# Squares of two row tiles and masks of a whole head pair at a time, six blocks by seven products, a ring of three, and copies off GpSimd, in a fused sparse attention and feed-forward kernel

**Chip and metric.** One core of one Trainium2 chip. Times are device microseconds (us) of whole executions; a profile's span runs from its first to its last instruction and is 1 to 2 us shorter.

## The reference

```python
# q, k, v: (8 batches, 8 heads, 576, 64);  w_in: (512, 2048);  w_out: (2048, 512)
scores = q @ k^T / 8                     # heads 0..3 see the last 32 positions ("loc"),
scores = where(mask[head], scores, -1e9) # heads 4..7 every 32nd one ("str")
x = (softmax(scores) @ v) as (4608, 512)
out = (s * relu(x @ w_in)**2 + b) @ w_out    # fp32
```

## The kernel before

All 4608 rows go through the feed-forward part in nine blocks T of 512. The first product (4 x 16 matmuls of 512 columns a block) gives a bank of PSUM for each of 16 row tiles; ScalarE takes the relu into `u`, VectorE squares it into `gT`. The second product comes in two forms: plain, 64 matmuls of 512 columns, or, from block `SEVEN` on, a 2 x 2 blocked product by seven products instead of eight, 112 matmuls of 256 columns, which needs sums of parts of `gT` (VectorE), mixed weights (made once) and more evictions. Attention of batch b runs between these matmuls and writes its transposed result into `xT`, a ring of `NX` batches.

A planner in Python simulates the engines when the program is built. It fixes the order of each engine's instructions, and for a copy it chooses the engine that it thinks will end first. Each `post` names what it needs, a cost in ns for each engine that may do it ("A" ScalarE, "V" VectorE, "P" GpSimd, "D" a transposing DMA), the function and the keys it sets. Each engine then works through its own instructions in that order; the GpSimd timeline of `e2_before_seven3` below shows a copy that stands behind DMA issues.

```python
LAT = {"A": 70.0, "V": 70.0, "P": 70.0, "D": 12000.0, ...}
...
eng = min(p[1], key=lambda e: max(self.free[e], r) + p[1][e])       # who ends first
...
    # scores of a bank: exponential, then its mask (84 masks in all)
    s.posts = [([key], {"A": 170 + 0.83 * 2 * n * nq}, ex, [("e", id_, g), group]),
               ([("e", id_, g)], {"V": 150 + 0.52 * 2 * n * nq}, ms, [("p", id_, g)])]
...
    # spreading q^T of the strided heads over qD_str
    plan.post([("qT", id_), ("s", (b - 1, m), 2)], {"P": 2000.0, "V": 940.0, "A": 1340.0},
              q_spread, [("q", id_)])
...
    # GpSimd issues the loads of batch b + 2; the plan counts no time for it
    plan.post([...], {"P": 0.0}, lambda eng, b=b: fetch_qk(b + 2), [("fetch", b + 2)])
    plan.post([...], {"P": 0.0}, lambda eng: fetch_v(b + 2), [("fetch_v", b + 2)])
```

The softmax here doesn't subtract the row's maximum and nothing guards it: scores larger than these inputs give would overflow.

## Time and profile before

| kernel before | |
|---|---|
| time | 311.52 us, median of 3 (311.32 to 311.59); profiled run 310.75, span 309.0 |
| busy: TensorE / VectorE / ScalarE / GpSimd | 97% / 71% / 58% / 32% |
| TensorE waits that the profile lists | 4.0 us, 2.6 of them before 21 us |

The prediction below shows and reads the profile's lines.

### The profile page before, as it was taken

The numbers are of one execution on the slowest core, as the hardware profiler recorded it, in microseconds if no ns is written. First come the engines' busy times: TensorE is split into PE (matmuls) and PEld (weight loads), VectorE is DVE, ScalarE is ACT, GpSimd is POOL, SyncE is SP. The second block draws the span as 40 slices with busy tenths as digits, with TensorE's granted clock in tenths as the row PEclk, the third lists the DMA queues.
The fourth block names the chain that finished last, engine by engine and source line by source line (L and its number), as shares of the span: only waits on it lengthen the run. The fifth ranks groups of instructions, "written<-read, shape, count | busy, mean of one in ns | idle before, by whom it ended". The sixth has DMA issues, their size and how long they took to land.

```text
span 309.0 us, 6715 instructions
## 1 busy us (share of the span) xinstructions
PE 300.5 (97%) x2526; PEld 194.4 (63%) x2526; DVE 218.2 (71%) x575; ACT 178.3 (58%) x336; POOL 99.8 (32%) x146
## 2 busy tenths in 40 slices
PE   8899999989999999999999999999999999999994
PEld 3765655555656655556687755565677666766883
DVE  7567958799976877859755874589866366737653
ACT  1876945769736964668055736694945445356300
POOL 8562559934951592059202950000000000000000
PEclk9999999999999999999999999999999999999999
DMA  7999999998999699679998999842010100200313
GB/s 127 204 212 205 216 175 159 219 135 122 99 165 176 86 147 155 110 110 183 150 174 153 128 146 159 172 92 88 2 36 34 68 2 34 104 1 0 105 67 106
DMA packets 99940, 37.28 MB, mean 121 GB/s; under 512 B 81170, under 2 KB 95890, under 8 KB 99906
## 3 DMA queue, kind: packets, MB, share of 16 engines
q0 software_dynamic: 57200, 18.08, 60.9%
q1 hardware_dynamic: 42706, 18.76, 29.9%
q8 instruction: 20, 0.33, 0.5%
q14 instruction: 14, 0.11, 0.1%
HBM read 36.84 MB, written 10.32 MB: 153 GB/s over the span
## 4 chain that ended last, share of the span: by engine, by line
PE 82%; DMA 9%; DVE 4%; issue 2%; ACT 1%; POOL 1%; SPq 0%; DVEq 0%; POOLq 0%; ACTq 0%
PE ps_f L877 35%; PE ps_f L926 20%; PE ps_f L845 12%; DMA ql<-in_q_dram 6%; PE ps_s L531 4%; PE ps_a L585 2%; DMA w_out_sb<-in_v_dram 2%; PE ps_s L845 2%; PE ps_t L585 1%; PE ps_t L845 1%; PE ps_s L926 1%; PE ps_t L411 1%; DMA out_dram<-o 1%; PE ps_t L633 1%; DVE gT L908 1%
## 5 line engine op out<-in xcount | busy, mean ns | idle before, releaser
L877 PE MATMUL ps_f<-xT,w_in_sb 128*128 128x512 f16 (+1 forms) x632 | 148.0, 357 | 0.0
L899 ACT ACTIVATE u<-ps_f 128x512 f16<-128x512 f32 x137 | 81.1, 596 | 72.8 <-PE ps_f L877 69.5
L877 PEld LDWEIGHTS <-w_in_sb 128*128 128x128 f16 x640 | 68.1, 113 | 34.5
L926 PE MATMUL ps_f<-w_out_sb,gT 128*128 128x512 f16 x304 | 80.7, 379 | 0.2 <-DVE gT L908 0.2
L908 DVE TENSOR_TENSOR gT<-u 128x512 f16<-128x512 f16 x111 | 48.1, 438 | 31.7 <-ACT u L899 30.6
L926 PEld LDWEIGHTS <-gT 128*128 128x128 f16 x320 | 28.9, 98 | 23.2 <-DVE gT L908 0.5
L845 PEld LDWEIGHTS <-gT 128*128 128x128 f16 x320 | 31.0, 98 | 8.7
L845 PE MATMUL ps_f<-w_out_sb,gT 128*128 128x256 f16 x184 | 25.9, 273 | 0.0
L611 DVE TENSOR_TENSOR x_nat<-ps_a,rec 72x256 f16<-72x256 f32 (+1 forms) x52 | 23.7, 456 | 0.6
L547 ACT ACTIVATE p_loc<-ps_s 128x384 f16<-128x384 f32 x46 | 21.1, 493 | 5.1 <-PE ps_s L531 4.8
L547 ACT ACTIVATE p_str<-ps_s 72x432 f16<-72x432 f32 (+1 forms) x46 | 21.0, 485 | 3.2 <-PE ps_s L531 2.9
L585 PEld LDWEIGHTS <-p_str 72*128 72x128 f16 x256 | 15.5, 98 | 11.2 <-issue 1.4
L906 ACT ACTIVATE gT<-u 128x512 f16<-128x512 f16 x33 | 20.8, 630 | 1.0
L293 POOL DMA_DIRECT2D v_loc<-in_v_dram x28 | 20.6, 764 | 1.8 <-DVE qD_loc L315 1.8
L937 DVE SCALAR_TENSOR_TENSOR o<-ps_f,s_sb,bcs 128x512 f32<-128x512 f32 x19 | 14.1, 747 | 9.4 <-PE ps_f L926 9.2
L298 POOL DMA_DIRECT2D v_str<-in_v_dram x16 | 13.0, 815 | 10.7 <-PE ps_a L585 3.7
L555 DVE TENSOR_TENSOR p_str<-p_str,mask_str 72x432 f16<-72x432 f16 (+1 forms) x42 | 14.7, 360 | 1.3 <-ACT p_str L547 1.0
L555 DVE TENSOR_TENSOR p_loc<-p_loc,mask_loc 128x384 f16<-128x384 f16 x42 | 14.6, 360 | 1.2 <-ACT p_loc L547 0.9
L845 PEld LDWEIGHTS <-S 128*128 128x128 f16 x128 | 12.5, 98 | 3.2
L315 ACT COPY xT<-ps_t 128x576 f16<-128x576 f16 x9 | 5.7, 637 | 13.4 <-PE ps_t L633 13.4
L600 DVE RECIPROCAL rec<-ps_a 72x4 f32<-72x4 f32 (+1 forms) x52 | 9.1, 176 | 6.1 <-PE ps_a L585 5.5
L585 PEld LDWEIGHTS <-p_loc 128*128 128x128 f16 x192 | 10.1, 98 | 5.2 <-issue 0.7
(158 smaller groups left out, 406.4 us busy)
## 6 DMA issues: line engine op xcount, KB each, us to landing
out_dram<-o SPq DMA_DIRECT2D x34, 256.0 KB, 3.1
w_out_sb<-in_moe_w_out_dram POOLq DMA_DIRECT2D x4, 512.0 KB, 11.1
v_loc<-in_v_dram POOLq DMA_DIRECT2D x28, 72.0 KB, 7.8
ql<-in_q_dram POOLq DMA_DIRECT2D x6, 288.0 KB, 6.4
qs<-in_q_dram POOLq DMA_DIRECT2D x6, 288.0 KB, 6.2
ks<-in_k_dram POOLq DMA_DIRECT2D x6, 288.0 KB, 7.6
kl<-in_k_dram POOLq DMA_DIRECT2D x4, 288.0 KB, 8.9
kl<-in_k_dram POOLq DMA_DIRECT2D x16, 72.0 KB, 3.9
```

Of the source, the lines that this page charges most:

```text
L293: nc.gpsimd.dma_start(out=vl[LPAD:128, h, :, 0:D], in_=v_band(b, h))
L547: nc.scalar.activation(out=pt[0:nk, 0:2 * n].rearrange("k t c -> k (t c)"), in_=st["s", g][0:nk, 0:2 * n * nq], func=AF.Exp, scale=scale)
L555: nc.vector.tensor_tensor(out=pt[0:nk, 0:2 * n], in0=pt[0:nk, 0:2 * n], in1=mask, op=ALU.mult)
L585: nc.tensor.matmul(out=st["a"][:, j % per, :], lhsT=st["pw", g][0:nk, i * nq:i * nq + WIDE], rhs=vt[0:nk, 2 * mm + e, j, :])
L611: nc.vector.tensor_tensor(out=st["x"][:, j0:j0 + per, 64 * e:64 * e + 64], in0=st["pa", e, j][0:nq, 0:per, 0:D], in1=st["rec", e, j][0:nq, ...
L845: nc.tensor.matmul(out=gts[name, T, t][:, 0] if halves else gts[name, T][:, t], lhsT=lhs(k, t), rhs=rhs(k), start=fresh and k == 0 and (ha ...
L877: nc.tensor.matmul(out=gts["h", T, ft][:, lo:hi], lhsT=w_in_sb[min(ft // 4, 2)][:, ct].rearrange("p (c x l) -> p c l x", x=128, l=4)[:, ma ...
L899: nc.scalar.activation(out=gts["u", T, ft], in_=gts["h", T, ft], func=AF.Relu)
L906: nc.scalar.activation(out=gts[T][:, ft, :], in_=u, func=AF.Square)
L908: nc.vector.tensor_tensor(out=gts[T][:, ft, :], in0=u, in1=u, op=ALU.mult)
L926: nc.tensor.matmul(out=gts[id_], lhsT=gts[T][:, ft, ts * 128:(ts + 1) * 128], rhs=w_out_sb[:, ft, cols], start=(ft == 0), stop=(ft == NFT ...
L937: nc.vector.scalar_tensor_tensor(out=o[:, 0:n], in0=gts[id_], scalar=s_sb[:, 0:1], in1=bcs[:, cols], op0=ALU.mult, op1=ALU.add)
```

## The change

Its intent: more blocks by seven products (fewer TensorE columns), and room on VectorE and in memory to do it. `SEVEN` goes from 5 to 3, so blocks 3 to 8. One square covers two row tiles, one mask a whole head pair. The ring shrinks to three batches, which pays for three `u` buffers of double size (a ring of four did not fit beside them). The plan counts GpSimd's time for issuing loads, and the pair copies may no longer go there. The plan's allowances for transposing DMAs in the first 110 us change as well.

```diff
-                self.done[k] = end + (6000.0 if soon else p[4] or
-                                           (5500.0 if eng == "D" and end < 110000.0 else self.LAT[eng]))
+                self.done[k] = end + (6000.0 if soon else p[4] or self.LAT[eng])
-    up = ctx.enter_context(tc.tile_pool(name="up", bufs=4))
+    up = ctx.enter_context(tc.tile_pool(name="up", bufs=3))
-    NX = 4
+    NX = 3
-        plan.post([key], {"A": 810, "V": 350, **({"P": 900.0} if b in (1, 2, 3) else {})}, g,
+        plan.post([key], {"A": 810, "V": 350}, g,
... masks: an exponential for each bank as before, then one multiply of 1152 elements
+                if b >= PE_MASK and g == ng - 1:
+                    s.posts.append(([("e", id_, x) for x in range(ng)],
+                                    {"V": 150 + 0.52 * 2 * nt * nq}, ms,
+                                    [("p", id_, x) for x in range(ng)]))
... xT of the loc heads
-                      [("xT", b, m)], 4000.0 if b == B - 1 else None)
+                      [("xT", b, m)], 4000.0 if b == B - 1 else 6000.0 if b < 4 else None)
-    SEVEN = 5
+    SQ_ACT = 0
+    SEVEN = 3
... squares: u is 128 x 2 x 512, one square for a pair, ScalarE may do it in every block
+                s.posts.append(([("u", T, x) for x in pair],
+                                {"V": 700, **({"A": 1055} if T >= SQ_ACT else {})}, sq,
+                                [("g", T, x) for x in pair]))
... GpSimd's issues
-                        {"P": 0.0}, lambda eng, b=b: fetch_qk(b + 2), [("fetch", b + 2)])
+                        {"P": 2900.0 + (2200.0 if b + 2 >= QB_DMA else 0.0)},
+                        lambda eng, b=b: fetch_qk(b + 2), [("fetch", b + 2)])
-                    [("fetch", b + 2)] + both("vs", b), {"P": 0.0}, lambda eng: fetch_v(b + 2),
+                    [("fetch", b + 2)] + both("vs", b), {"P": 3600.0}, lambda eng: fetch_v(b + 2),
```

More of the change, by code (lines that the diff above doesn't have):

```diff
@@ L199 @@
     WIDE = 128
-    p_bufs = {True: [const.tile([128, 3 * LQ + WIDE], FP16, name=f"p_loc{i}") for i in range(6)],
-              False: [const.tile([SQ, 5 * SQ + WIDE], FP16, name=f"p_str{i}") for i in range(6)]}
+    p_bufs = {True: [const.tile([128, 11 * LQ + WIDE], FP16, name=f"p_loc{i}") for i in range(2)],
+              False: [const.tile([SQ, 15 * SQ + WIDE], FP16, name=f"p_str{i}") for i in range(2)]}
     p_taken = {True: 0, False: 0}
@@ L254 @@
     for tl in p_bufs[True]:
-        nc.vector.memset(tl[:, 4 * LQ:], 0.0)
+        nc.vector.memset(tl[:, 12 * LQ:], 0.0)
     for tl in p_bufs[False]:
-        nc.vector.memset(tl[:, 4 * SQ:], 0.0)
+        nc.vector.memset(tl[:, 16 * SQ:], 0.0)
     loaded = {}
@@ L539, in score @@
                 s.keys = [key]
+                ng = nt // per_s + (nt % per_s > 0)
                 def ex(eng):
-                    whole = p_bufs[loc][p_taken[loc] % len(p_bufs[loc])]
-                    p_taken[loc] += 1
-                    st["pw", g] = whole
-                    pt = whole[:, 0:2 * per_s * nq].rearrange("k (t c) -> k t c", c=nq)
-                    st["pt", g] = pt
+                    if g == 0:
+                        st["whole"] = p_bufs[loc][p_taken[loc] % len(p_bufs[loc])]
+                        p_taken[loc] += 1
+                    at = g * 2 * per_s * nq
+                    st["pw", g] = st["whole"][:, at:]
                     nc.scalar.activation(
-                        out=pt[0:nk, 0:2 * n].rearrange("k t c -> k (t c)"),
+                        out=st["pw", g][0:nk, 0:2 * n * nq],
                         in_=st["s", g][0:nk, 0:2 * n * nq], func=AF.Exp, scale=scale)
                 def ms(eng):
-                    pt = st["pt", g]
+                    pt = st["whole"][:, 0:2 * nt * nq].rearrange("k (t c) -> k t c", c=nq)
                     mask = (mask_loc if loc else mask_str)[:, None, :].to_broadcast(
-                        [nk, 2 * n, nq])
-                    nc.vector.tensor_tensor(
-                        out=pt[0:nk, 0:2 * n], in0=pt[0:nk, 0:2 * n], in1=mask, op=ALU.mult)
-                s.posts = [([key], {"A": 170 + 0.83 * 2 * n * nq}, ex, [("e", id_, g), group]),
-                           ([("e", id_, g)], {"V": 150 + 0.52 * 2 * n * nq}, ms,
-                            [("p", id_, g)])]
-                if b < PE_MASK:
-                    s.posts = [([key], {"A": 170 + 0.83 * 2 * n * nq}, ex, [("p", id_, g), group])]
+                        [nk, 2 * nt, nq])
+                    nc.vector.tensor_tensor(out=pt[0:nk], in0=pt[0:nk], in1=mask, op=ALU.mult)
+                free = [("a", (b - 1, m), 1, nt - 1)] if b else []
+                s.posts = [([key] + free, {"A": 170 + 0.83 * 2 * n * nq}, ex,
+                            [("p" if b < PE_MASK else "e", id_, g), group])]
+                if b >= PE_MASK and g == ng - 1:
+                    s.posts.append(([("e", id_, x) for x in range(ng)],
+                                    {"V": 150 + 0.52 * 2 * nt * nq}, ms,
+                                    [("p", id_, x) for x in range(ng)]))
             return s
@@ L894, in ff1 @@
             s.keys = [key] + ([("F1", T)] if ft == NFT - 1 else [])
+            at = ff_order(T).index(ft)
+            pair = tuple(ff_order(T)[at // 2 * 2:at // 2 * 2 + 2])
             def rl(eng):
-                gts["u", T, ft] = up.tile([128, PS], FP16, tag="u", name="u")
+                if at % 2 == 0:
+                    gts["u", T, pair] = up.tile([128, 2, PS], FP16, tag="u", name="u")
+                u = gts["u", T, pair][:, at % 2]
                 if eng == "A":
-                    nc.scalar.activation(out=gts["u", T, ft], in_=gts["h", T, ft], func=AF.Relu)
+                    nc.scalar.activation(out=u, in_=gts["h", T, ft], func=AF.Relu)
                 else:
-                    nc.vector.tensor_relu(out=gts["u", T, ft], in_=gts["h", T, ft])
+                    nc.vector.tensor_relu(out=u, in_=gts["h", T, ft])
             def sq(eng):
-                u = gts["u", T, ft]
+                u = gts["u", T, pair]
+                g = gts[T][:, pair[0]:pair[0] + 2, :]
                 if eng == "A":
-                    nc.scalar.activation(out=gts[T][:, ft, :], in_=u, func=AF.Square)
+                    nc.scalar.activation(out=g, in_=u, func=AF.Square)
                 else:
-                    nc.vector.tensor_tensor(out=gts[T][:, ft, :], in0=u, in1=u, op=ALU.mult)
-            at = ff_order(T).index(ft)
-            free = ([("g", T, ff_order(T)[at - 4])] if at >= 4 else
-                    [("g", T - 1, ff_order(T - 1)[at - 4])] if T else [])
-            s.posts = [([key] + free, {"A": 600, **({"V": 690} if T == 0 else {})}, rl, [("u", T, ft), group]),
-                       ([("u", T, ft)], {"V": 430, **({"A": 600} if T >= SEVEN else {})}, sq, [("g", T, ft)])]
+                    nc.vector.tensor_tensor(out=g, in0=u, in1=u, op=ALU.mult)
+            first = at // 2 * 2
+            free = ([("g", T, ff_order(T)[first - 6])] if first >= 6 else
+                    [("g", T - 1, ff_order(T - 1)[first - 6])] if T else [])
+            s.posts = [([key] + free, {"A": 600, **({"V": 690} if T == 0 else {})}, rl, [("u", T, ft), group])]
+            if at % 2:
+                s.posts.append(([("u", T, x) for x in pair],
+                                {"V": 700, **({"A": 1055} if T >= SQ_ACT else {})}, sq,
+                                [("g", T, x) for x in pair]))
         return s
```

## The prediction

> **What bounds the kernel now.** I read the page's first part, then the busy time by stretch, then the waits of TensorE alone, then the chain that ended last and the groups kept apart by form.
>
> The busy time by stretch (columns: TensorE matmuls, weight loads, VectorE, ScalarE, GpSimd, each with its count, then the granted clock, the DMA share and GB/s):
>
> ```profile
> PE 300.5 (97%) x2526; PEld 194.4 (63%) x2526; DVE 218.2 (71%) x575; ACT 178.3 (58%) x336; POOL 99.8 (32%) x146
> ...
> 60.00:90.00 30.00, 28.57 (x254) 17.09 (x254) 27.62 (x73) 22.12 (x46) 19.57 (x27) 1.00 1.07 132
> 90.00:130.00 40.00, 40.00 (x351) 23.59 (x350) 30.63 (x100) 25.16 (x49) 14.25 (x23) 1.00 1.39 141
> 130.00:220.00 90.00, 90.00 (x692) 56.90 (x689) 63.45 (x179) 54.55 (x105) 27.55 (x40) 1.00 1.21 135
> 220.00:300.00 80.00, 80.00 (x582) 58.10 (x580) 50.75 (x88) 38.51 (x64) 0.00 (x0) 1.00 0.12 40
> ```
>
> TensorE is busy without a break from 90 to 300 us. It loses 1.43 us between 60 and 90 us, where VectorE is 92% busy. A busy TensorE is not by itself a TensorE at its peak, so I check the pace. In the chain that ended last, its pieces are start, length, what:
>
> ```profile
> 118.11 2.16 PE ps_f L926 x10
> ...
> 236.53 4.04 PE ps_f L845 x37
> ```
>
> A matmul with 512 columns takes 2.16/10 = 0.216 us and one with 256 columns 4.04/37 = 0.109 us, start to start. Both are the column count over 2.4 GHz plus 2 to 3 ns (the clock is granted whole, 1.00), so there is nothing to gain but fewer columns. What TensorE waits for, over the whole span (total, times, longest):
>
> ```profile
> PE ps_f L1162 <- DVE w_mix L243: 1.1, 1, 1.1
> PE ps_t L411 <- DVE qD_str L315: 0.7, 1, 0.7
> PE ps_a L585 <- DVE x_nat L611: 0.5, 2, 0.3
> ...
> PE ps_s L531 <- DVE kTs L315: 0.4, 1, 0.4
> PE ps_f L1162 <- DVE x_nat L611: 0.4, 1, 0.4
> PE ps_f L926 <- DVE gT L908: 0.2, 1, 0.2
> ```
>
> The sum is under 5 us in a span of 309, more than half of it in the first 21 us. So **TensorE's column count sets the time**; VectorE (71%) and ScalarE (58%) count only where they make it wait. The rows that price their work:
>
> ```profile
> L908 DVE TENSOR_TENSOR gT<-u 128x512 f16<-128x512 f16 x111 | 48.1, 438 | 31.7 <-ACT u L899 30.6
> ...
> L906 ACT ACTIVATE gT<-u 128x512 f16<-128x512 f16 x33 | 20.8, 630 | 1.0
> ...
> L555 DVE TENSOR_TENSOR p_loc<-p_loc,mask_loc 128x384 f16<-128x384 f16 x42 | 14.6, 360 | 1.2 <-ACT p_loc L547 0.9
> ...
> L937 DVE SCALAR_TENSOR_TENSOR o<-ps_f,s_sb,bcs 128x512 f32<-128x512 f32 x19 | 14.1, 747 | 9.4 <-PE ps_f L926 9.2 <-ACT bcs L971 0.2
> ...
> L717 DVE TENSOR_TENSOR gT<-gT 128x1024 f16<-128x1024 f16 x16 | 10.7, 685 | 0.9 <-PE ps_f L845 0.4 <-ACT gT L906 0.4
> ...
> L787 DVE TENSOR_TENSOR Ub<-Ua,bcs 128x512 f32<-128x512 f32 x4 | 2.8, 692 | 0.1
> ```
>
> The last number before the second bar is the mean of one in ns. VectorE's multiply of 512 halves costs 438 ns and its subtraction of 1024 costs 685: doubling the size adds 247, so 190 ns of each is fixed. That fixed part is what the pairing of squares and masks saves.
>
> **What the Trainium skill says.** "TensorE: Matmul & The Clock Gate", Back-to-back issue gap, gives N/2.4 + 2.5 ns for a lone matmul on a warm array, but says a stream with weight loads may go otherwise (131 ns at N=512). This trace, a stream with a weight load for each matmul, follows the lone formula: 216 against 215.8, 109 against 109.2. "VectorE: DVE Perf Modes", The perf-mode tier table, has `tensor_tensor` in 16 bits at two elements a cycle, 0.52 ns an element at 0.96 GHz; the trace's slope is 247/512 = 0.48. The same page's rules say to minimize op count; the 190 ns agree. "ScalarE: Activation LUTs", What ACT_TABLE_LOAD costs, has 186 ns + 0.833 ns an element, 612 ns for 512; the square from memory takes 630 here. "SBUF — State Buffer", Who interferes with whom, says that a VectorE operation with two inputs in SBUF contends with a GpSimd instruction that reads SBUF. The rows of the masks and squares agree in kind: medians of 350 and 425 ns, with single ones at 777 and 1036. No row here proves the cause.
>
> **The change, part by part.** The count of instructions comes from the two built programs' orders.
>
> *Six blocks by seven products instead of four.* In the second product, 128 matmuls of 512 columns go (320 to 192) and 224 of 256 columns come (448 to 672): −128 × 0.2163 + 224 × 0.1092 = −27.69 + 24.46 = **−3.23 us** of TensorE. On VectorE each such block adds 8 sums of 1024 (8 × 0.686 = 5.5 us) and has 7 evictions and one addition (7 × 0.75 + 0.69 = 5.9) instead of 4 evictions (3.0): two blocks give +11.0 and +5.9 us. The four mixed weight tiles are made some 60 us earlier.
>
> *xT a ring of three.* The wrap falls inside two blocks (192+320 and 384+128 columns) and no longer inside one (256+256). By the formula above the four pieces take 82.5 + 135.8 + 162.5 + 55.8 = 436.6 ns, 64 times, 27.94 us; before it was 64 × 216.3 + 128 × 109.2 = 27.82. **+0.1 us**, an estimate.
>
> All other matmuls are the same in number and size, also the attention's and the filling ones at the start. TensorE: **−3.1 us**.
>
> *Squares of two rows.* VectorE has 50 of 1024 in place of 111 of 512: 111 × 0.438 − 50 × 0.687 = 48.6 − 34.4 = −14.2 us. ScalarE has 22 of 1024 in place of 33: by its slope of 0.83 each is some 1.05 us (estimate), 23.1 − 20.8 = +2.3.
>
> *Masks of a head pair.* 28 of 1152 elements in place of 84 small ones (29.3 us by the two groups). Extrapolated, one is 360 + 768 × 0.48 = 0.73 us, or by the steeper slope of the mask rows up to 0.88; I take 0.80: 22.4, so −6.9 us. In exchange the first product with V waits for all scores of its pair: one full mask, 0.8 us, where it had needed a third of it.
>
> *Copies.* GpSimd loses 4 pair copies and 6 of qD_str, some 8 us. VectorE gains some 3 us of copies net (4 more of qD_loc from PSUM, fewer of xT), ScalarE some 3 (6 more of qD_str).
>
> Sum for VectorE: 11.0 + 5.9 − 14.2 − 6.9 + 3 − about 2 (8 fewer clears of p buffers, one relu) = −3 us: about 215 of 308, no relief over the whole but a shift, lighter before 130 us, heavier from 130 to 220, where the two new blocks run beside attention. There it has 63 of 90 us now; +17 +5 (weights) −6 (half of its squares and masks) makes some 79, 88%. ScalarE: about 184. Neither becomes the bound.
>
> **On the path:** only TensorE's −3.1 us, and its waits. Of the 1.4 us lost at 60 to 90 us, where VectorE was 92% busy, I expect about half back (masks and squares lighter, DMA allowances longer): −0.7. For the new load at 130 to 220 us I allow +0.5. Start and tail: the last products and evictions stand in the same order in both programs. 311.5 − 3.1 − 0.7 + 0.5 = **308.2 us**.
>
> **The rivals.**
> 1. *VectorE takes TensorE's place in 130 to 220 us.* For it: 88% by my sum, and at 92% it did make TensorE wait 1.4 us in 30. Two PSUM banks carry seven products with evictions between them. Against it: at 220 to 300 us the same seven products run with no TensorE wait, and attention gives TensorE more to choose from. It would give back 1 to 5 us: 309 to 313.
> 2. *The longer latency of the mask.* One more 0.4 us on 28 pairs, if all of it shows: +11 us. Against it: in the order of the new program at least 1.6 us of other matmuls (priced as above) stand between a pair's last score and its first product with V, and in most pairs over 3; the last exponential and the mask need some 1.3. I expect under 1 us: 309.
> 3. *The ring of three holds attention up.* The transposed rows of a batch may land only when the first layer has finished with the batch three back. Priced by TensorE work, batch 7's rows are made at 190 to 205 us, the block that frees them ends at 193, and they are first read after 220. The margin of some 25 us exceeds the 9.3 us of a landing. Worth 0.
> 4. *More gain:* all waits of 20 to 90 us vanish: 308.4 − 2 = 306.5.
>
> **Range and chances.** The column count is sure to some tenths; the waits spread from −2 to +2, with a longer tail upwards for rival 1: **306.6 to 310.2**. Faster by over 2% needs under 305.4, more than all waits outside the start could give: 0.03. Slower by over 2% needs over 317.7, +9 us of new waits: 0.03. Within 2%: 0.94.
>
> **What would show it right or wrong.** Right: 512-column and 256-column matmuls still 216 and 109 ns apart in the chain; TensorE unbroken from 90 us to the tail; squares of 1024 at 0.69 us and masks of 1152 at 0.73 to 0.88 us; VectorE's total within 5 us of 215. Wrong: waits of TensorE on x_nat, gT, S or w_mix between 130 and 220 us that add to over 2 us (rival 1); waits of the products with V on the mask (rival 2); of the first layer on xT (rival 3); or pieces of 128 columns at much more than 56 ns, as a weight load for each of them might make.

## The result

**308.38 us** (median of 4, 307.81 to 309.19) against 311.55 for the kernel before (4 runs): ratio 0.9895, 95% interval 0.9863 to 0.9928. A ratio here is the mean time of one kernel's fast runs over that of the other's fast runs of the same rounds, so not quite the ratio of the medians. The interval is clear of 1.

The changed kernel's first page line and its busy time by stretch (columns as in the prediction):

```profile
PE 297.2 (97%) x2686; PEld 206.0 (67%) x2686; DVE 217.5 (71%) x479; ACT 183.9 (60%) x330; POOL 93.8 (31%) x136
...
60.00:90.00 30.00, 28.70 (x270) 17.50 (x269) 27.45 (x62) 24.86 (x49) 15.38 (x22) 1.00 1.21 146
130.00:220.00 90.00, 90.00 (x806) 65.70 (x804) 70.64 (x159) 59.57 (x106) 28.05 (x40) 1.00 1.13 132
220.00:300.00 80.00, 79.87 (x611) 60.31 (x609) 48.55 (x73) 32.38 (x50) 0.00 (x0) 1.00 0.13 44
```

TensorE is as full as before with less work. VectorE's total stayed (217.5 against 218.2), and between 130 and 220 us it rose from 63 to 71 us of 90 without making TensorE wait. Between 220 and 300 us one wait of 0.13 us is new. Between 60 and 90 us TensorE still loses 1.30 us, where it had lost 1.43. Three groups kept apart by form, and three pieces of the chain that ended last:

```profile
L917 DVE TENSOR_TENSOR gT<-u 128x1024 f16<-128x1024 f16 x50 | 34.4, 687 | 23.9 <-ACT u L907 23.4
L915 ACT ACTIVATE gT<-u 128x1024 f16<-128x1024 f16 x22 | 23.3, 1057 | 0.6
L556 DVE TENSOR_TENSOR p_loc<-p_loc,mask_loc 128x1152 f16<-128x1152 f16 x14 | 10.3, 744 | 2.8 <-ACT p_loc L548 2.7
```

```profile
159.81 2.59 PE ps_f L880 x12
...
213.94 1.31 PE ps_f L880 x12
...
234.95 4.04 PE ps_f L848 x37
```

Squares, masks and matmul pace came as estimated: 687, 1057 and 744 ns; 0.216 us for 512 columns (2.59/12), 0.109 for 256 (4.04/37). In the block that the ring splits into 384 + 128 columns, twelve matmuls take 1.31 us, 218 ns for such a pair: the formula's 162.5 + 55.8, so the short ones are not slowed by their weight loads.

**The start differs from run to run.** TensorE's first matmul of the second product starts at 39.3 us in the profile of before and at 40.9 here, because the loads of the second batch's q landed later (TensorE waits listed for `ql` and `qs`). That is not the change's doing alone: the kernel of `e2_before_seven3` below has the same TensorE order as the kernel before until far past this point, and started its second product at 41.3:

```profile
L926 PE MATMUL ps_f<-w_out_sb,gT x304: 377/379/389, 39.3 to 212.9; 128*128 128x512 f16 x152
```

```profile
L938 PE MATMUL ps_f<-w_out_sb,gT x176: 377/379/390, 40.9 to 151.2; 128*128 128x512 f16 x176
```

```profile
L926 PE MATMUL ps_f<-w_out_sb,gT x176: 377/379/390, 41.3 to 151.0; 128*128 128x512 f16 x176
```

(First the kernel before, then the changed kernel, then that experiment; "39.3 to 212.9" is first and last start.) The two profiled runs themselves differ by only 1.9 us (310.75 and 308.83). So I also compare the stretch from that matmul's start to the start of the last one: 265.1 us before, 261.9 after, 3.2 less, which is the column count's 3.1.

### The profile page after: what moved, and what is told of

The parts are those of the page before. It is cut to its first block, busy times and chain, and to the rows that moved or that the text cites. A ratio compares the mean times of both kernels' runs of the same rounds, so it can differ in the third digit from the quotient of the medians.

```text
span 307.1 us, 6883 instructions
## 1 busy us (share of the span) xinstructions
PE 297.2 (97%) x2686; PEld 206.0 (67%) x2686; DVE 217.5 (71%) x479; ACT 183.9 (60%) x330; POOL 93.8 (31%) x136
## 4 chain that ended last, share of the span: by engine, by line
PE 85%; DMA 9%; DVE 3%; POOL 1%; issue 1%; ACT 0%; SPq 0%; POOLq 0%
PE ps_f L880 36%; PE ps_f L848 20%; PE ps_f L938 12%; DMA qs<-in_q_dram 4%; PE ps_s L530 4%; PE ps_a L587 2%; DMA w_out_sb<-in_v_dram 2%; DMA ql<-in_q_dram 2%; PE ps_s L848 2%; PE ps_t L410 2%; PE ps_t L587 1%; PE ps_t L848 1%; PE ps_s L938 1%; PE ps_t L635 1%; DVE qD_str L314 1%
## 5 line engine op out<-in xcount | busy, mean ns | idle before, releaser
L880 PE MATMUL ps_f<-xT,w_in_sb 128*128 128x512 f16 (+4 forms) x696 | 148.1, 340 | 0.1
L848 PEld LDWEIGHTS <-gT 128*128 128x128 f16 x512 | 49.1, 98 | 11.5
L917 DVE TENSOR_TENSOR gT<-u 128x1024 f16<-128x1024 f16 x50 | 34.4, 687 | 23.9 <-ACT u L907 23.4
L938 PE MATMUL ps_f<-w_out_sb,gT 128*128 128x512 f16 x176 | 47.9, 379 | 0.5 <-DVE gT L917 0.3
L848 PE MATMUL ps_f<-w_out_sb,gT 128*128 128x256 f16 x312 | 43.4, 273 | 0.0
L938 PEld LDWEIGHTS <-gT 128*128 128x128 f16 x192 | 17.1, 98 | 12.7 <-DVE gT L917 1.1
L915 ACT ACTIVATE gT<-u 128x1024 f16<-128x1024 f16 x22 | 23.3, 1057 | 0.6
L587 PEld LDWEIGHTS <-p_str 72*128 72x128 f16 x256 | 15.5, 98 | 8.7 <-issue 1.1
L720 DVE TENSOR_TENSOR gT<-gT 128x1024 f16<-128x1024 f16 x28 | 18.5, 683 | 2.6 <-ACT gT L915 1.3
L848 PE MATMUL ps_f<-w_mix,gT 128*128 128x256 f16 x144 | 18.3, 273 | 0.0
L720 DVE TENSOR_TENSOR S<-gT 128x1024 f16<-128x1024 f16 x16 | 10.6, 685 | 5.6 <-PE ps_f L848 4.5
L848 PE MATMUL ps_f<-w_mix,S 128*128 128x256 f16 x96 | 13.7, 272 | 0.0
```

The costliest lines, as they stand in the source:

```text
L587: nc.tensor.matmul(out=st["a"][:, j % per, :], lhsT=st["pw", g][0:nk, i * nq:i * nq + WIDE], rhs=vt[0:nk, 2 * mm + e, j, :])
L720: nc.vector.tensor_tensor(out=at(out), in0=at(x), in1=at(y), op=op)
L848: nc.tensor.matmul(out=gts[name, T, t][:, 0] if halves else gts[name, T][:, t], lhsT=lhs(k, t), rhs=rhs(k), start=fresh and k == 0 and (ha ...
L880: nc.tensor.matmul(out=gts["h", T, ft][:, lo:hi], lhsT=w_in_sb[min(ft // 4, 2)][:, ct].rearrange("p (c x l) -> p c l x", x=128, l=4)[:, ma ...
L915: nc.scalar.activation(out=g, in_=u, func=AF.Square)
L917: nc.vector.tensor_tensor(out=g, in0=u, in1=u, op=ALU.mult)
```

## The experiments

Two theories stood at the start. *Columns*: TensorE's column count alone moved the time, the other parts are neutral. *A (relief)*: VectorE had to be relieved first, and the paired squares and masks are worth something. Theory *C* (GpSimd's queue) was formed after the first four runs. All experiments ran against the kernel before in the same rounds (5 rounds each), and all gave correct results.

| run | what it is | median us | ratio, 95% interval |
|---|---|---|---|
| e1_seven5 | change, seven products at 4 blocks | 311.80 | 1.0004 (0.9980 to 1.0028) |
| e2_before_seven3 | before, seven products at 6 blocks | 321.96 | 1.0316 (1.0287 to 1.0345) |
| e3_single_masks | change, masks single | 307.44 | 0.9866 (0.9843 to 0.9889) |
| e4_single_squares | change, squares single | 307.68 | 0.9875 (0.9858 to 0.9893) |
| e5_seven3_poolcost | e2 + GpSimd's issue costs | 310.22 | 0.9955 (0.9913 to 0.9996) |
| e6_no_poolcost | change without issue costs, copies on GpSimd allowed | 320.44 | 1.0298 (1.0262 to 1.0333) |
| e7_seven2 | change, seven products at 7 blocks | 309.94 | 0.9952 (0.9924 to 0.9979) |
| e8_seven1 | change, seven products at 8 blocks | 313.32 | 0.9958 (0.9931 to 0.9985) |
| e9_both_single | change, masks and squares single | **306.06** | 0.9827 (0.9804 to 0.9850) |
| e10_ring4 | e9 with a ring of four | 307.32 | 0.9859 (0.9832 to 0.9885) |
| e11_short_allowance | change, old DMA allowances | 308.16 | 0.9892 (0.9870 to 0.9915) |
| e12_after_again | the changed kernel again | 308.39 | 0.9913 (0.9884 to 0.9942) |

e1 to e4, e5 to e8 and e9 to e12 shared a chip and rounds each.

### Undo or do the seven products alone

```diff
e1, in the changed kernel        e2, in the kernel before
-    SEVEN = 3                   -    SEVEN = 5
+    SEVEN = 5                   +    SEVEN = 3
```

> The changed kernel with the seven products back at four blocks (all else of the change kept). Theory (only TensorE's column count moved the time): the 3.23 us come back and the ring's split stays, so 311.5 to 311.7 us, ratio to before 1.000. Rival A (the paired squares and masks and the lighter VectorE are worth something on their own): under 310.5. Rival B (the new masks' latency costs something that the columns hide): over 312.5.

> The kernel before with the seven products at six blocks, nothing else. Theory: TensorE's matmuls fall by 3.23 us and nothing else matters, 308.2 to 308.6 us. Rival A (VectorE must be relieved first; this kernel adds 17 us to it with single squares and masks): new waits of TensorE on x_nat, gT or S between 130 and 220 us worth 1 to 4 us, so 309.5 to 312.

e1 came as the column theory has it: 311.8 us, the gain is gone. That says that the other parts come to nothing together, not that each does nothing; the last experiments show that some do something. (One of its six runs, the profiled one, took 634 us. It is set aside as slow.) e2 agreed with neither theory: not 308 and not 309.5 to 312, but **322**. The longest of its waits of TensorE (total, times, longest):

```profile
PE ps_s L531 <- POOL qD_str L315: 10.3, 1, 10.3
```

GpSimd around that wait (start, length, what; in brackets its own idle time before it):

```profile
169.95 0.40 POOL L997 COPY gate<-kT 1x1 f16<-1x1 f16 x1 [0.52 <-DMA kT<-ks]
170.50 2.99 POOL L270 DMA_DIRECT2D ql<-in_q_dram  x4 [0.15 <-DVE gT L908]
173.48 2.89 POOL L270 DMA_DIRECT2D kl<-in_k_dram  x4
...
177.79 2.94 POOL L293 DMA_DIRECT2D v_loc<-in_v_dram  x4
...
185.24 0.80 POOL L298 DMA_DIRECT2D v_str<-in_v_dram  x1 [1.57 <-DMA ks<-in_k_dram]
186.04 1.39 POOL L315 COPY qD_str<-qT 64x576 f16<-64x576 f16 x2
```

A copy of 1.4 us stands behind 15.5 us of DMA issues and their waits, and TensorE's next scores need it. The plan had counted those issues at 0 ns, so GpSimd looked free, and it placed two copies there at this point. The kernel before has the same zero; its other qD_str copies on GpSimd fall into gaps. It got away with it until `SEVEN` moved the order.

The loss closes. From the second product's start to the last matmul the kernel before takes 265.1 us; less 3.2 for the columns, plus 10.3 for the wait and 3.0 for the clock after it make 275.2, and e2's profile has 275.3. The 3.0 come from matmuls at half the clock for 6.0 us. Two stretches after the wait:

```profile
187.50:194.00 6.50, 6.50 (x43) 5.10 (x43) 3.25 (x9) 1.98 (x4) 0.00 (x0) 0.54 2.18 40
194.00:200.00 6.00, 6.00 (x56) 4.38 (x54) 4.37 (x12) 2.29 (x4) 1.22 (x2) 1.00 0.52 138
```

The granted clock is 0.54 on average in the first 6.5 us (0.50 until 193.5 us) and 1.00 after it. The Trainium skill, "TensorE: Matmul & The Clock Gate", What's actually happening, says that an idle window of about 3.4 us halves TensorE's clock until it has been busy for about as long. The halving agrees with this trace; the lengths do not quite: the clock fell 2.7 us after the last matmul and came back 6.0 us after the matmuls resumed (5.8 us in e6).

### One part of the rest undone at a time

e3 puts one mask for each bank and the six small p buffers back; e4 one square for each row tile, with four `u` buffers.

> The changed kernel with the masks back at one per bank of scores and six small p buffers. Theory: 308.4 us, no difference. Rival A (VectorE's load, +8.7 us here, is near the bound): 309.5 or more. Rival B (the pair's longer latency costs): under 307.7, with the waits on x_nat at 82 to 87 us gone.

> The changed kernel with one square for each row tile, four u buffers, squares on ScalarE only from the fourth block on. Theory: 308.4 us, no difference. Rival A (VectorE's load, some +14 us here): 309.5 to 312 with waits of TensorE on gT, S and x_nat between 60 and 220 us.

Neither costs anything: 307.4 and 307.7 us. Relief in either form is not needed. e3's time even falls where its rival B (the pair's longer latency costs) had put it, under 307.7, but its interval overlaps that of the changed kernel. Nothing yet says whether one of them must be there.

### GpSimd's costs in the plan

```diff
e5: the kernel before with SEVEN = 3 and
-                        {"P": 0.0}, lambda eng, b=b: fetch_qk(b + 2), [("fetch", b + 2)])
+                        {"P": 2900.0 + (2200.0 if b + 2 >= QB_DMA else 0.0)},
+                        lambda eng, b=b: fetch_qk(b + 2), [("fetch", b + 2)])
-                    [("fetch", b + 2)] + both("vs", b), {"P": 0.0}, ...
+                    [("fetch", b + 2)] + both("vs", b), {"P": 3600.0}, ...
e6: the changed kernel with these lines and the pair copies' "P" turned back
```

> The kernel before with six blocks by seven products (as in e2_before_seven3, 322.0 us) and, of the rest of the change, only GpSimd's issue costs in the plan (2900 and 5100 ns for q and k, 3600 for v, in place of 0). It places one copy less on GpSimd, the qD_str copy that stood behind the issues there; the order of the other GpSimd copies is as before. Theory C (the 10.3 us of e2 are that one queueing, and the column count does the rest): the 10.3 us wait is gone, 308.2 to 309 us. Rival A (VectorE must be relieved): over 310, with waits of TensorE on x_nat, gT or S.

> The changed kernel with pair copies allowed on GpSimd again and its issue costs back to 0. The plan then puts two late qD_str copies and three early pair copies on GpSimd. Theory C: if those two stand behind DMA issues, a wait of some 5 to 15 us on POOL qD_str for one of them, 312 to 320 us; if they fall into a gap, 308.4. Rival D (this part does nothing): 308.4 whatever their place.

e6 confirms C from the other side: without this part the changed kernel takes 320.4 us, and its longest wait is on the same copy:

```profile
PE ps_s L530 <- POOL qD_str L314: 11.6, 1, 11.6
```

In e5 the 10.3 us are gone, and with them all but 1.8 us of e2's loss against the changed kernel. It is not the whole story: its runs lie in two groups (308.9 to 309.2 and 311.3 to 312.2), and the profile, of the second group, has new waits:

```profile
PE ps_a L585 <- DVE x_nat L611: 1.7, 2, 1.4
PE ps_s L531 <- DMA kT_alt<-kl: 1.5, 1, 1.5
PE ps_f L877 <- ACT u L899: 0.9, 2, 0.8
```

In the timeline kT_alt's transposes are issued only at 190.5 us (184.1 in e10 below), and GpSimd still spreads qD_loc in 1.7 us at 193; what made them late I did not separate. That leaves rival A open, and the pair copies and the allowances.

### More blocks by seven products

e7 has `SEVEN = 2`, e8 `SEVEN = 1`, both in the changed kernel.

> The changed kernel with seven blocks by seven products. Theory (columns): another 64 x 216.3 - 112 x 109.2 = 1.6 us less, 306.8 us. Rival A: the additional block runs at 90 to 130 us beside attention; VectorE is 71% busy there and gets 8.5 us more of 40, 93%: new waits, 307.5 to 310.

> The changed kernel with all blocks but the first by seven products. Theory (columns): 3.2 us less, 305.2 us. Rival A: the second block's second product runs at 55 to 105 us, where VectorE is 91% busy already between 60 and 90; mixed weights (5 us) and sums come on top: new waits of 3 to 8 us, 308 to 313. One qD_str copy of the second batch stands on GpSimd here: a wait on it would be theory C again.

Fewer columns, and slower. e7 has 1.6 us less TensorE work than the changed kernel and takes some 1.5 us more. Its profile has a wait that the other had not, at 152 us, beside attention:

```profile
PE ps_f L848 <- DVE Va L767: 1.6, 1, 1.6
```

The second product of a seven-product block may go on only when VectorE has read the first (`Va`). In its queue stood attention's multiplies and two sums (1.28 us). Here VectorE does become the limit, as rival A says, though only in single places: it is busy 72.8 us of 90 between 130 and 220, and 33.6 of 40 between 90 and 130. The loss is not where the expectation had put it: TensorE loses 2.01 us between 130 and 220 us and 0.38 between 90 and 130. e8's runs fell into three fast ones at 310.3 to 310.6, three slow ones at 316 to 317 (its profile among these), so only its ratio, from the fast runs, is used: no better than e7.

### Squares and masks both single

The decisive one for rival A: the changed kernel with **both** back to single operations, so VectorE has more work than in the changed kernel. e10 adds a ring of four, which then fits; e11 turns the allowances back in the changed kernel; e12 is the changed kernel again.

```diff
e10: the same as e9, and         e11: the changed kernel, and
-    NX = 3                      -   end + (6000.0 if soon else p[4] or self.LAT[eng])
+    NX = 4                      +   end + (6000.0 if soon else p[4] or
                                 +          (5500.0 if eng == "D" and end < 110000.0 else self.LAT[eng]))
                                 and x_dma's 6000.0 for b < 4 taken out
```

> The changed kernel with masks and squares both back to single operations (six blocks by seven, ring of three, GpSimd's costs and the copies' places, the transposes' longer allowances kept). VectorE gets some 20 us more work than in the changed kernel. Rival A (the relief of VectorE is what makes six blocks possible, and either of the two halves of it is enough, which e3 and e4 alone could not show): 309.5 to 312 us with waits on x_nat, gT, Va. Theory C (only the columns and GpSimd's placing count): 307.4 to 308.5 us.

> As e9 with xT a ring of four (it fits when the u and p buffers are the small ones). It differs from e5 only in the pair copies and in the transposes' allowances. Theory: as e9, less the 0.1 us of the split, within 0.3 us. If the ring of three costs waits: 0.5 us or more faster than e9.

> The changed kernel with the plan's allowance for a transposing DMA before 110 us back at 5.5 us (12 us in the change, 6 for the first blocks' xT). If the allowance is what avoids the waits that e5 still has: waits on a transpose's landing or on copies behind it before 110 us, 309 to 311. If not: 308.4.

> The changed kernel itself once more, on the same chip and in the same rounds as e9 to e11, to tell whether the 307.4 and 307.7 us of e3 and e4 are better than it: 308.0 to 308.8 us as before if so, 307.4 to 307.9 if the difference was the chip's or the rounds'.

e9 is the fastest kernel, **306.06 us**, 1.7% under the kernel before, and its interval lies clear of the changed kernel's in the same rounds (0.9804 to 0.9850 against 0.9884 to 0.9942). That is below what either theory expected (C: 307.4 to 308.5). Rival A falls: the pairing was not needed, and with it the kernel is slower. Why it is slower is not shown. The stretch of 60 to 90 us, first in e9, then in e12:

```profile
60.00:90.00 30.00, 29.57 (x264) 17.68 (x262) 26.43 (x77) 24.80 (x50) 14.73 (x20) 1.00 1.30 144
```

```profile
60.00:90.00 30.00, 29.21 (x274) 17.87 (x273) 27.15 (x63) 25.23 (x49) 14.89 (x21) 1.00 1.26 141
```

e9 loses 0.43 us of TensorE there, e12 0.79 and the first profile of the changed kernel 1.30. Over the whole span VectorE is busy 222.7 us in e9 and 217.5 in the changed kernel: **5 us more work and less waiting**. One way in which pairs may cost something stands in the timeline of the changed kernel (TensorE's transpose of x_nat waits for VectorE):

```profile
82.22 0.69 DVE L917 TENSOR_TENSOR gT<-u 128x1024 f16<-128x1024 f16 x1
...
82.93 0.72 DVE L556 TENSOR_TENSOR p_loc<-p_loc,mask_loc 128x1152 f16<-128x1152 f16 x1
...
83.57 0.41 DVE L613 TENSOR_TENSOR x_nat<-ps_a,rec 72x256 f16<-72x256 f32 x1
...
84.04 0.30 PE L635 MATMUL ps_t<-ident,x_nat 72*128 72x72 f16 x4 [0.46 <-DVE x_nat L613]
```

A pair's square and a pair's mask, 1.4 us in two pieces, stand ahead of the 0.41 us that TensorE needs, and it waits 0.46 us. That this is what makes e9 faster is argued only, and the record speaks against it as the main cause: near the same place e9 has a wait of 0.35 us on x_nat, the kernel before, all single, lost 1.43 us in this stretch, and e6, all paired, loses the least of all, 0.23:

```profile
60.00:90.00 30.00, 29.77 (x274) 18.24 (x272) 26.67 (x61) 24.58 (x48) 18.62 (x26) 1.00 1.06 144
```

Little of the 2.3 us between e9 and e12 lies in this stretch or after it. From the first matmul of the second product to the last matmul e9 takes 260.9 us, e12 261.2, the first profile of the changed kernel 261.9: 0.3 to 1.0 us. But e11, paired too, takes 261.0, and e4, with single squares, 262.1, so this does not single the pairs out. Most of the profiles' 2.0 us lies in the start (39.9 against 41.3), where the profiles differ by when q landed. e10, whose TensorE order is e9's there, started the second product at 40.6 and took 260.9 from then on, which leaves 307.3 us and shows that the start alone can make 1 us. Whether paired squares make a late start likelier is open: their order differs before that point too. The profiles hint at it: with paired squares (the change, e3, e6, e7, e11, e12) the second product starts at 40.8 to 42.0 us, with single ones (before, e4, e5, e9, e10) at 39.3 to 40.6, though at 41.3 in e2.

The ring of three costs nothing (e9 is not slower than e10, which differs from it only there; e10 came 1.3 us slower, where 0.3 was expected, and the profiles put that into the start and the tail). The allowances alone do nothing in the changed kernel (e11 308.2, e12 308.4). e5 (310.2; ratio 0.9913 to 0.9996) and e10 (307.3; 0.9832 to 0.9885) differ in the pair copies and the allowances together: by the ratios (the two ran on different chips) these two are worth some 3 us, as much as the columns. Which of them takes e5's waits away was not separated; e11 points to the copies, but in another kernel.

## Why the prediction was right, step by step

- **Range and size.** 308.2 predicted, 308.4 measured, inside the range. The sum was partly right by balance, which is luck: the copies and allowances, which the sum has only inside its −0.7, gave some 3 us (e5 to e10), e2's order would have cost 13, and the pairing took 2 (e9 to e12). The next points show the rest.
- **"TensorE's column count sets the time", −3.23 and +0.1 us.** Right. The pace held for every form; the stretch from the second product's start to the end shrank by 3.2 us; undoing only this part (e1) gives the time of before. As a statement that the columns are *all* that counts it was wrong: e2 has the same columns and takes 322 us.
- **The step "Copies", taken as a shift of some 8 us off GpSimd.** This was the step that failed, though it did not show in the sum. I priced the copies' own time and not the queue they stand in. GpSimd is 32% busy, and I did not ask what stands before a copy there; but it spends up to 16 us at a time issuing loads, in order (e2), and a copy behind them cost TensorE 10.3 and 11.6 us (e2, e6) and then its clock. Counting the issues is what made six blocks possible (e2 against e5, e6 against the change). None of my four rivals named it.
- **"I expect about half back: −0.7" for 60 to 90 us.** Undecided: the loss went from 1.43 to 1.30 us in the first profile of the changed kernel, to 0.79 in the second (e12). Two profiles of one kernel differ by as much as the gain. The reasons given are not borne out: e9, with more VectorE work, loses only 0.43, and e11, with the old allowances, 0.85.
- **"+0.5" for the heavier VectorE between 130 and 220 us.** It cost 0: TensorE is busy 90.00 of 90. VectorE had 71 us there, not the 79 I had summed. By the two traces the sums and evictions added the 17 us; but the weights added 0.4 us and not 5, since the kernel before mixes its weights in the same stretch, and the squares and masks fell by 9.9 us and not 6. The mechanism of rival 1 is seen one block further (e7, 1.6 us on `Va`).
- **Rival 2, the mask's latency:** no wait on a mask appears. **Rival 3, the ring:** worth 0, as said (e10). **Start and tail:** I said that they stay; the tail did, the start moves by up to 2 us from run to run (39.3 and 41.3 with the same order), which the three runs I had did not show.

## What to carry to other kernels

In a planned order, every engine's queue must carry its true costs, also an engine's time for issuing DMAs: here 1.4 us of copies behind a row of issues cost 10 to 12 us, and then TensorE's clock as well. When TensorE is the bound, less work on a helper engine may be worth nothing by itself: 5 us less on VectorE came with 2 us more in all (e12 against e9). And undo the parts of a bundle singly and together: here the gain came from the columns, the counted issues, and the copies and allowances, and two others (paired squares and masks) were better left out. e1 alone would have called all but the columns neutral.

## What the Trainium skill lacked or had wrong

- "TensorE: Matmul & The Clock Gate", Back-to-back issue gap, gives 131 ns a matmul for N=512 and 81 ns for N=128 in a stream with weight loads. Here such streams run at 216 ns for 512 columns, 109 for 256, and 218 for a pair of 384 and 128, which leaves 56 for 128 if the 384 take the formula's 162.5: the page's own lone-matmul formula, not its stream figures.
- "DMA: Bandwidth & Descriptors", SWDGE vs HWDGE vs iDMA, says that GpSimd computes the descriptors in software. I found no warning there of what that does to other GpSimd work: an issue took 0.7 to 0.8 us, a batch of loads kept the queue for 15.5 us, and a 1.4 us copy behind it held TensorE up for 10.3 us.
- "VectorE: DVE Perf Modes", Rules for kernel authors, says to minimize the number of operations. That holds for VectorE's own busy time here (222.7 us with 580 instructions in e9, 217.5 with 479 in the change), but not for the kernel, which TensorE bounds: 306.06 us against 308.39.
